# Reordering two stage boundaries in a fused adaLN + spectral mixer + MLP backward kernel

## The chip, the cores and the metric

The kernel runs on one core of one Trainium2 chip. The metric is device time in microseconds of one execution, the median of three runs. The engines are named as the profile names them: PE (matrix products), DVE (elementwise and reductions), ACT (activations and PSUM evacuation), POOL and SP (here mostly issuers of DMA). The program is written in Tile: instructions are traced in Python order, a planner puts them into one fixed order per engine from its own estimates, and every engine then runs its list in that order, waiting on semaphores. `issue_after(x)` forces instructions behind x in the list of their engine.

## The reference, cut to what matters

The forward pass is a conditioned block of two halves, and the kernel computes its output and the gradients of nine inputs. Sizes: 2048 tokens (S), 1024 channels (D), 3584 hidden (F), bf16.

```python
def _fwd_reference(A_x, A_w_r, A_w_i, B_x, B_w1, B_b1, B_w2, B_b2, c, w_mod):
    # A: rfft2 over (tokens, channels), times w_r + i w_i, irfft2
    # B: layernorm, gelu(y @ w1 + b1) @ w2 + b2
    ...
    mod = (_silu(c) @ w_mod).reshape(c.shape[0], 6, 1, -1)
    sa, ca, ga, sb, cb, gb = (mod[:, 0].copy(), ...)
    h = _layernorm(x, axis=-1) * (1 + ca) + sa
    x = x + ga * _A_ref(h, A_w_r, A_w_i)
    h = _layernorm(x, axis=-1) * (1 + cb) + sb
    x = x + gb * _B_ref(h, B_w1, B_b1, B_w2, B_b2)
    return x

def reference(..., grad_out):
    _out, _vjp = jax.vjp(_f, A_x, A_w_r, A_w_i, B_w1, B_b1, B_w2, B_b2, c, w_mod)
    return (_out, *_vjp(grad_out))
```

## The kernel before, in words

Tokens are worked on in four groups of 512, called frames or quarters here (b = 0 to 3), each held as four tiles of 128 tokens. All weights and the large intermediates pass through on-chip buffers that are named by a tag (`px0` to `px5`, `sma`, `smb`, `t0` to `t3`, `uv0` to `uv3`, `fr`, `ot`, `wt`, `ph`, `gm`, `sb`); a tag has one buffer, and a new tile of that tag waits until every reader of the old one is done. PSUM has the tags s and d (two banks each) and f (four banks).

The stages in order: modulation rows; the forward spectral mixer; the MLP, forward and its inner gradient; the backward of the second LayerNorms; the backward of the spectral mixer, with the weight gradients of w2 and w1 filled in as spare work for PE; the last sums.

The MLP works frame by frame. `z_block` (L795) forms the hidden pre-activations, applies gelu and its derivative, and stores two arrays to HBM: `d_hh` (hidden activations) and `d_gz` (gradient of the pre-activations). `bo_pass` (L836) multiplies by w2, in two column halves of seven steps each; a step is 16 matmuls and one w2 block of 512 KB, loaded into a ring of four buffers (`w2p`, L831). After the seventh step the four sums (`pbo`) are evacuated by ACT (L845), DVE forms the output and a product `go`, and PE sums it over tokens (`pa`, L855) into `gacc`. A plan written by hand sets PE's order here, and `ordered()` keeps it. The z blocks of a frame run among the steps of the frame before, so frame 3 has w2 steps alone. When frame 3 is done, `gacc` is reduced (`pq`, L903), stored as row 5 of the modulation gradient, and a ring of eight steps (`gmod_ring((5,))`, L958 and L960) turns it into one part of the gradient of w_mod.

The first boundary of this document, called seam 1, lies here. The next stage needs w1 transposed: seven tiles `w1T`, loaded by 28 transposing DMAs on SP (L973), each into the buffer of a spent w1 tile. Then, for every frame (L1002 to L1053 of the loop `for b in range(NB)`): load `n3u`, `n2u`, four tiles of grad_out (`go4`) and seven blocks of `gz` (L1013, a ring of eight buffers); the product `pg` = gz x w1T (L1020) in two column halves, evacuated by ACT into `gn3` (L1025, two buffers, so PE may be one frame ahead); then on DVE `ln_bwd` over `n3u` (L919 to L924), column sums of `gn3` and `pru` on PE (`sums3`), `ln_bwd` over `n2u`, adding `go4`, which gives g2. g2 is stored to `d_gx1` from POOL (L1046), multiplied by the ga row into `n3u`, folded over tokens and channels by eight half-width additions and subtractions into one quarter of `fbuf2`, and multiplied by `au` (a load of `d_A`) for another column sum, `sums3_ga` (L195).

The second boundary, seam 2, follows frame 3: four tiles `gB` = grad_out x gb row are loaded and multiplied (into `px2` to `px5`, the buffers of w1T tiles 0 to 3). Then `pieces()` hands out PE work: for each of 28 blocks of hidden units a transposing load of `d_hh` (L1139, two ahead) and two products gw2 (L1114) of 16 matmuls over all 16 token tiles, evacuated and stored as the gradient of w2; later the gradient of w1. `fill(n)` runs the next n of them: 16 of them stand before the spectral backward, whose first matmul is `pu` (L470) and needs all of `fbuf2`.

Of the kernel before, what the change touches and what calls it, by code (L numbers as in the profile page):

```python
# [14 lines left out]
ALU = mybir.AluOpType  # L15
# [20 lines left out]
def kernel(  # L36
# [69 lines left out]
    d_gx1 = dram.tile([S, D], BF16, name="d_gx1")  # L106
    d_ph = dram.tile([F, S], BF16, name="d_ph")
# [712 lines left out]
    w2n = [0]  # L820

    def bo_pass(b, h):
        cs_ = slice(h * KH, (h + 1) * KH)
        pbs = [(ps_f if b < NB - 1 or h == 0 else (ps_s, ps_d)[k % 2])("pbo") for k in range(4)]
        for i in range(4):
            with ordered():
                last_pe[0] = nc.tensor.matmul(pbs[i][:], lhsT=ones_bf[0:1, :], rhs=b2_row[0:1, cs_], start=True, stop=False)
        for g in range(7):
            wp = w2p[w2n[0] % 4]
            w2n[0] += 1  # L830
            nc.sync.dma_start(out=wp, in_=w2_v[:, g * 4:(g + 1) * 4, cs_])  # L831
            hh = hh_slots[(b * 7 + g) % 11]
            for i in range(4):
                for k in range(4):
                    with ordered():
                        last_pe[0] = nc.tensor.matmul(pbs[i][:], lhsT=hh[:, k, i * P:(i + 1) * P], rhs=wp[:, k, :],  # L836
                                                      start=False, stop=(g == 6 and k == 3))
# [12 lines left out]

        yield
        pa = (ps_d if b < NB - 1 else ps_f)("pa")
        for i in range(4):
            with ordered():
                last_pe[0] = nc.tensor.matmul(pa[32 * i:32 * (i + 1), :], lhsT=ones_bf[:, 0:32], rhs=go[:, i, :], start=True, stop=True)  # L855
# [42 lines left out]
    for late in bo_late:  # L898
        next(late, None)
    g5 = []  # L900
    for h in range(2):
        pq = (ps_s, ps_d)[h]("pq")
        nc.tensor.matmul(pq[0:1, :], lhsT=quad[:], rhs=gacc[:, h * KH:(h + 1) * KH], start=True, stop=True)  # L903
        g5.append(pq[0:1, :])
    store_gmod(g5, 5)

    gb1 = small.tile([P, NFC], FP32, tag="gb1", bufs=1)
    nc.vector.reduce_sum(out=gb1[:], in_=gb1_acc[:], axis=AX.X)
    gb1_bf = small.tile([P, NFC], BF16, tag="b1_bf", bufs=1)
    nc.vector.tensor_copy(out=gb1_bf[:], in_=gb1[:])  # L910
    fin = reg.tile([P, 2, P], BF16, name="fin", tag="gm")
    make_identity(nc, fin[:, 0, :])
    to_rows(fin[0:NFC, 1, :], gb1_bf[:], NFC, fin[:, 0, :])
    nc.sync.dma_start(out=out_5.rearrange("(f p) -> f p", p=P), in_=fin[0:NFC, 1, :])


    def ln_bwd(g_in, gsum, n_ap, rstd, out_ap, tmp):
        sc = small.tile([P, 4], FP32, tag="lbsc", bufs=4)
        nc.vector.tensor_tensor_reduce(out=tmp, in0=g_in, in1=n_ap, scale=1.0, scalar=0.0,  # L919
                                       op0=ALU.mult, op1=ALU.add, accum_out=sc[:, 1:2])  # L920
        nc.vector.tensor_scalar(out=sc[:, 2:3], in0=gsum, scalar1=rstd, scalar2=-1.0 / D, op0=ALU.mult, op1=ALU.mult)
        nc.vector.tensor_scalar(out=sc[:, 3:4], in0=sc[:, 1:2], scalar1=rstd, scalar2=-1.0 / D, op0=ALU.mult, op1=ALU.mult)
        nc.scalar.activation(out=tmp, in_=n_ap, func=ACT.Identity, scale=sc[:, 3:4], bias=sc[:, 2:3])
        nc.vector.scalar_tensor_tensor(out=out_ap, in0=g_in, scalar=rstd, in1=tmp, op0=ALU.mult, op1=ALU.add)  # L924
# [43 lines left out]
    w1Ts = []  # L968
    for g in range(7):
        wtile = reg.tile([P, 4, D], BF16, name=f"w1T_{g}", tag=W1T[g])  # L970
        for k in range(4):
            fc = g * 4 + k
            nc.sync.dma_start_transpose(out=wtile[:, k, :], in_=B_w1[:, fc * P:(fc + 1) * P])  # L973
        w1Ts.append(wtile)
    gzr = [reg.tile([P, 2, 4, BW], BF16, name=f"gzr{k}", tag=f"t{k}") for k in range(4)]
    gn3s = [reg.tile([P, 4, D], BF16, name="gn3a", tag="uv0"), reg.tile([P, 4, D], BF16, name="gn3b", tag="wt")]
    n3u = reg.tile([P, 4, D], BF16, name="n3u", tag="uv1")
    n2u = reg.tile([P, 4, D], BF16, name="n2u", tag="uv2")
    pru = reg.tile([P, 4, D], BF16, name="pru", tag="uv3")[:]
# [3 lines left out]
    gzn = 0  # L983
    gmw = reg.tile([P, 2, D], BF16, name="gmw", tag="ph")
    gmg = reg.tile([P, 2, D], BF16, name="gmg", tag="sb")
    early = gmod_ring((5,), [gmw[:, 0], gmw[:, 1], gmg[:, 0]], gmg[:, 1, :])
    next(early)
    au = reg.tile([P, 4, D], BF16, name="au", tag="px1")

    fold2_in = {}  # L990
# [9 lines left out]

    for b in range(NB):
        gn3 = gn3s[b % 2]  # L1002
        sums = small.tile([P, 2, 4], FP32, tag="sums")
        gzt = []
        nc.sync.dma_start(out=n3u[:], in_=chunk_rows(d_n3, b))
        nc.sync.dma_start(out=n2u[:], in_=chunk_rows(d_x1, b))
# [3 lines left out]
        for g in range(7):  # L1010
            sl = gzr[gzn % 8 // 2][:, gzn % 2]
            gzn += 1
            nc.sync.dma_start(out=sl, in_=d_gz_v[:, g * 4:(g + 1) * 4, b * BW:(b + 1) * BW])  # L1013
            gzt.append(sl)
        for h in range(2):
            pgs = [ps_f("pg") for _ in range(4)]
            for g in range(7):
                for i in range(4):
                    for k in range(4):
                        nc.tensor.matmul(pgs[i][:], lhsT=gzt[g][:, k, i * P:(i + 1) * P],  # L1020
                                         rhs=w1Ts[g][:, k, h * KH:(h + 1) * KH],
                                         start=(g == 0 and k == 0), stop=(g == 6 and k == 3))
            for i in range(4):
                with tc.high_priority():
                    nc.scalar.activation(out=gn3[:, i, h * KH:(h + 1) * KH], in_=pgs[i][:], func=ACT.Identity,  # L1025
                                         accum_out=sums[:, h, i:i + 1])
# [4 lines left out]
        next(early, None)  # L1031
# [12 lines left out]
        next(early, None)  # L1044
        tt(g2[:], g2[:], go4, ALU.add)
        nc.gpsimd.dma_start(out=chunk_rows(d_gx1, b), in_=g2[:])  # L1046
        nc.sync.dma_start(out=au[:], in_=chunk_rows(d_A, b))
        tt(n3u[:], g2[:], bcn(ga_row, 4), ALU.mult)
        fold_tok(n3u, ftmp)
        fold2_in[b] = fold_d(fbuf2[:, b], n3u[:], ftmp)  # L1050
        tt(au[:], g2[:], au[:], ALU.mult)
        if b < NB - 1:
            sums3_ga(b, au)  # L1053
            next(early, None)
# [3 lines left out]
    gBs = []  # L1058
    for b in range(NB):
        gb_t = reg.tile([P, 4, D], BF16, name=f"gB{b}", tag=PXT[2 + b])  # L1060
        gb_in = load_tok(gb_t, grad_out, b)
        with tc.high_priority():
# [15 lines left out]
    hh_o = [4, 5, 6, 7] * 2 + [0, 1] + [2, 0, 1] * 6  # L1078
# [32 lines left out]
    gwo = reg.tile([P, 2, D], BF16, name="gwo", tag="ph")  # L1111

    def gw2_mm(acc, fc, h, t):
        nc.tensor.matmul(acc[:], lhsT=hh_s[hh_o[fc]][:, t, :], rhs=gBs[t // 4][:, t % 4, h * KH:(h + 1) * KH],  # L1114
                         start=(t == 0), stop=(t == NT - 1))

    def gw2_out(acc, fc, h):
        with tc.high_priority():
            nc.any.tensor_copy(out=gwo[:, fc % 2, h * KH:(h + 1) * KH], in_=acc[:])  # L1119
        if h == 1:  # L1120
            nc.gpsimd.dma_start(out=out_6[fc * P:(fc + 1) * P, :], in_=gwo[:, fc % 2])

    w1g = {}
    hh_in = [None]
# [12 lines left out]
    def pieces():  # L1137
# [3 lines left out]
        hh_load(0)  # L1141
        yield
        hh_load(1)
        for fc in range(NFC):
            if fc + 2 < NFC:
                hh_load(fc + 2)
            for h in range(2 if fc < NFC - 2 else 0):
                acc = ps_f("gw2acc")
                for t in range(NT):
                    gw2_mm(acc, fc, h, t)  # L1150
                gw2_out(acc, fc, h)
# [38 lines left out]
    done = [0]  # L1190
# [6 lines left out]
    next(todo)  # L1197
    with tc.issue_after(gb_in.ins):
        fill(6)
# [81 lines left out]
```

## Time and profile before

| | us |
|---|---|
| median of 3 runs (1502.69 to 1513.5) | 1510.4 |
| the profiled execution | 1507.2 |
| its span in the trace | 1505.0 |
| PE busy | 1408.0 (94%) |
| DVE busy | 1068.8 (71%) |
| ACT busy | 721.4 (48%) |
| POOL busy | 371.6 (25%) |
| mean granted TensorE clock | 0.978 |
| last w2 step of the MLP begins | 768.0 |
| first `pg` matmul | 777.8 |
| last `pg` matmul ends, about | 988.9 |
| first `pu` matmul | 1062.6 |

The profile is one execution. It is read as a page of totals, and by queries of its trace: who waited for whom, the instructions in order of time, and the busy time of each engine in a stretch. An entry `x<-y` names what an instruction writes and reads; the bracket behind a timeline row is the idle time of the engine ahead of it and what ended that. Stretches with a clock under 1.00 are those in which PE had been idle.

### The profile page before, as it was taken

The page shows a single profiled execution, that of the slowest core. Times are in us where ns is not written, and L with a number is a line of the kernel's source. Part 1 is how long each engine was busy: PE and PEld are TensorE (multiplying, and loading weights), DVE is VectorE, ACT ScalarE, POOL GpSimd, SP SyncE. Part 2 cuts the span into 40 slices and gives each one's busy share as a digit, 9 for nine tenths or more (in the row PEclk, how much of TensorE's full clock was granted, in tenths as well). Part 3 has the DMA queues.
Part 4 walks back from the last instruction along what each step waited for, and adds up shares of the span by engine and source line. Part 5 has one row for each costly group of instructions (what it writes and reads, how often), then busy time and mean ns, then how long its engine had stood idle before and what let it go on. Part 6 is the DMA issues. An engine that isn't in the chain of part 4 may idle for free.

```text
span 1505.0 us, 18218 instructions
## 1 busy us (share of the span) xinstructions
PE 1408.0 (94%) x6703; PEld 655.0 (44%) x6835; DVE 1068.8 (71%) x1574; ACT 721.4 (48%) x960; POOL 371.6 (25%) x427
## 2 busy tenths in 40 slices
PE   5899989999999999999889999969999999899998
PEld 2434545444444444444334444424454444444443
DVE  5883777898799888877413877959067776997551
ACT  4765446757887755666111433313532344453211
POOL 5710631210112122212112001220124421222432
PEclk8999999999999999999999999989999999999999
DMA  9982664899687777899956246398379987675992
GB/s 336 265 223 67 156 212 137 264 245 338 225 252 230 233 243 231 247 279 262 344 195 221 76 180 224 107 214 211 98 188 241 248 221 222 175 198 149 275 294 92
DMA packets 358168, 324.27 MB, mean 215 GB/s; under 512 B 209191, under 2 KB 300861, under 8 KB 357824
## 3 DMA queue, kind: packets, MB, share of 16 engines
q1 hardware_dynamic: 324192, 207.71, 51.3%
q0 software_dynamic: 33888, 115.41, 22.5%
q8 instruction: 53, 0.87, 0.2%
q14 instruction: 35, 0.29, 0.1%
HBM read 164.15 MB, written 109.10 MB: 182 GB/s over the span
## 4 chain that ended last, share of the span: by engine, by line
PE 42%; DVE 19%; DMA 8%; issue 6%; ACT 5%; POOL 1%; SPq 0%; POOLq 0%; DVEq 0%; ACTq 0%
PE pbo L836 10%; PE pz L795 10%; PE gw2acc L1114 8%; PE gw1acc L1181 4%; PE pg L1020 4%; DVE ct L172 4%; DVE got L919 2%; PE pu L470 2%; PE pv L563 2%; ACT ct L460 1%; DVE gn3a L924 1%; DVE st L436 1%; DMA gB<-in_grad_out_dram 1%; DMA n3u<-d_n 1%; DMA w2sA<-in_B_w_dram 1%
## 5 line engine op out<-in xcount | busy, mean ns | idle before, releaser
L678 PE MATMUL pp<-gBoT,wt 128*128 128x512 bf16 x878 | 198.2, 383 | 4.9 <-DMA wt<-in_B_w_dram 2.0
L1020 PE MATMUL pg<-w1T,gzr 128*128 128x512 bf16 x876 | 195.2, 381 | 1.5 <-issue 0.7
L1181 PE MATMUL gw1acc<-gzh,n3n 128*128 128x512 bf16 x876 | 195.0, 381 | 1.1 <-issue 0.2
L678 PEld LDWEIGHTS <-wt 128*128 128x128 bf16 x896 | 88.0, 98 | 110.0 <-issue 6.1
L795 PEld LDWEIGHTS <-w 128*128 128x128 bf16 x896 | 87.5, 98 | 109.4 <-issue 6.0
L1020 PEld LDWEIGHTS <-gzr 128*128 128x128 bf16 x896 | 87.0, 98 | 108.5 <-issue 6.0
L1181 PEld LDWEIGHTS <-n3n 128*128 128x128 bf16 x896 | 87.6, 98 | 105.9 <-issue 2.4
L795 PE MATMUL pz<-n3Ta,w 128*128 128x512 bf16 x437 | 99.5, 383 | 2.9 <-ACT gt L798 2.1
L1114 PE MATMUL gw2acc<-gB,hhsA 128*128 128x512 bf16 x437 | 97.9, 379 | 1.0 <-DMA hhsA<-d_hh 0.4
L795 PE MATMUL pz<-n3Tb,w 128*128 128x512 bf16 x439 | 98.4, 379 | 0.5
L1119 ACT CAST gwo<-gw2acc 128x512 bf16<-128x512 f32 x54 | 30.5, 584 | 130.1 <-PE gw2acc L1114 84.1
L836 PEld LDWEIGHTS <-hhA 128*128 128x128 bf16 x608 | 58.9, 98 | 75.2 <-issue 5.1
L798 ACT ACTIVATE gt<-pz,b_col 128x512 bf16<-128x512 f32 x112 | 73.1, 683 | 35.6 <-PE pz L795 33.7
L1185 ACT CAST gwo<-gw1acc 128x512 bf16<-128x512 f32 x53 | 30.8, 582 | 115.1 <-PE gw1acc L1181 91.6
L804 ACT ACTIVATE gt<-gt 128x2048 bf16<-128x2048 bf16 x28 | 53.5, 1910 | 66.1 <-DVE gt L172 66.0
L172 DVE TENSOR_TENSOR gt<-gt,gt 128x2048 bf16<-128x2048 bf16 x56 | 68.5, 1223 | 21.6 <-ACT gt L806 20.9
L172 DVE TENSOR_TENSOR ct<-ct 128x2048 bf16<-128x2048 bf16 x64 | 75.9, 1221 | 10.3 <-ACT ct L631 9.0
L1114 PE MATMUL gw2acc<-gB,hht 128*128 128x512 bf16 x251 | 58.6, 393 | 14.4 <-DMA hht<-d_hh 10.3
L1114 PEld LDWEIGHTS <-hhsA 128*128 128x128 bf16 x448 | 43.6, 98 | 52.5 <-DMA hhsA<-d_hh 0.9
L800 ACT ACTIVATE gt<-gt 128x2048 bf16<-128x2048 bf16 x28 | 53.4, 1907 | 0.6
L806 ACT ACTIVATE gt<-gt 128x2048 bf16<-128x2048 bf16 x28 | 53.4, 1907 | 0.5
L1186 POOL DMA_DIRECT2D out_dram<-gwo x56 | 30.5, 546 | 84.5 <-ACT gwo L1185 74.3
(313 smaller groups left out, 2495.2 us busy)
## 6 DMA issues: line engine op xcount, KB each, us to landing
gzr<-d_gz SPq DMA_DIRECT2D x28, 512.0 KB, 6.4
wblk<-in_w_mod_dram SPq DMA_DIRECT2D x12, 1024.0 KB, 9.7
d_ph<-pho POOLq DMA_DIRECT2D x21, 512.0 KB, 5.6
out_dram<-otl POOLq DMA_DIRECT2D x40, 256.0 KB, 3.6
d_hh<-hhA POOLq DMA_DIRECT2D x19, 512.0 KB, 4.8
w2sD<-in_B_w_dram SPq DMA_DIRECT2D x14, 512.0 KB
hhC<-d_ph SPq DMA_DIRECT2D x14, 512.0 KB, 4.9
w2sA<-d_ph SPq DMA_DIRECT2D x14, 512.0 KB, 4.5
```

The costliest lines, as they stand in the source:

```text
L172: return nc.vector.tensor_tensor(out=out, in0=a, in1=b, op=op)
L678: last_pe[0] = nc.tensor.matmul(pp[:], lhsT=wt[:, fg % 2, cch, k * P:(k + 1) * P], rhs=gBoT[j][:, cch, :], start=(cch == 0), stop=(cch == ...
L795: last_pe[0] = nc.tensor.matmul(pz[:], lhsT=w1s[g][:, cch, k * P:(k + 1) * P], rhs=n3T[:, cch, :], start=(cch == 0), stop=(cch == NDC - 1))
L798: nc.scalar.activation(out=zb[:, k, :], in_=pz[:], func=ACT.Identity, bias=b1_col[:, fc:fc + 1], scale=1.0)
L800: nc.scalar.activation(out=av, in_=zb, func=ACT.Square)
L804: nc.scalar.activation(out=sg, in_=bv, func=ACT.Sigmoid, scale=2.0 * GK)
L806: nc.scalar.activation(out=bv, in_=bv, func=ACT.Sigmoid, scale=-2.0 * GK)
L836: last_pe[0] = nc.tensor.matmul(pbs[i][:], lhsT=hh[:, k, i * P:(i + 1) * P], rhs=wp[:, k, :], start=False, stop=(g == 6 and k == 3))
L1020: nc.tensor.matmul(pgs[i][:], lhsT=gzt[g][:, k, i * P:(i + 1) * P], rhs=w1Ts[g][:, k, h * KH:(h + 1) * KH], start=(g == 0 and k == 0), sto ...
L1114: nc.tensor.matmul(acc[:], lhsT=hh_s[hh_o[fc]][:, t, :], rhs=gBs[t // 4][:, t % 4, h * KH:(h + 1) * KH], start=(t == 0), stop=(t == NT - 1))
L1181: nc.tensor.matmul(acc[:], lhsT=n3ns[t // 4][:, t % 4, cch * P:(cch + 1) * P], rhs=gz2[t // 8][:, t % 8, :], start=(t == 0), stop=(t == NT ...
L1185: nc.any.tensor_copy(out=ob, in_=acc[:])
```

## The change

Four things are altered, all between the last MLP frame and the spectral backward.

Seam 1: the w2 loads of the last frame are issued three steps ahead; the transposes of w1T from number 8 on and the gz blocks of frame 0 are tied behind given w2 loads on SP; the `pg` product of frame 0 is written as two generators and its steps follow the last w2 step in PE's fixed order, the second column half in the s and d banks of PSUM, with the late `pa`, the `pq` reduction and the whole row-5 ring of the modulation gradient between them.

The frame loop: the ga product and the fold work in place in g2, not in `n3u`; the `au` column sum of a frame is issued on PE behind the next frame's `pg`; `gn3a` and `pru` exchange buffers (`uv3`, `uv0`).

gB: each frame multiplies its `go4` by the gb row once it is no longer needed. For frames 0 and 1 the product goes to a new HBM array `d_gB` and is loaded again at the end of frame 2, for frames 2 and 3 it goes straight into the tiles that the gw2 products read.

Seam 2: the first two transposed hh tiles are loaded into the quarter of `fbuf2` that the last frame will fill, and their four products run on PE directly behind the last `pg`.

```diff
+    d_gB = dram.tile([2 * BW, D], BF16, name="d_gB")
...
+    def w2_load(upto):
+        while len(w2_in) <= min(upto, NB * 14 - 1):
+            n = len(w2_in)
+            h, g = n // 7 % 2, n % 7
+            w2_in.append(nc.sync.dma_start(out=w2p[n % 4], in_=w2_v[:, g * 4:(g + 1) * 4, h * KH:(h + 1) * KH]))
...
-            wp = w2p[w2n[0] % 4]
-            w2n[0] += 1
-            nc.sync.dma_start(out=wp, in_=w2_v[:, g * 4:(g + 1) * 4, cs_])
+            n = (2 * b + h) * 7 + g
+            w2_load(n + 3 if b == NB - 1 else n)
+            wp = w2p[n % 4]
...
-        pa = (ps_d if b < NB - 1 else ps_f)("pa")
+        pa = (ps_f if (b, h) == (NB - 1, 0) else ps_d)("pa")
...
+    def behind_w2(k):
+        return tc.issue_after(w2_in[(NB - 1) * 14 + min(max(k, 0), 13)].ins)
+
+    for g in range(7):
+        wtile = reg.tile([P, 4, D], BF16, name=f"w1T_{g}", tag=W1T[g])
+        for k in range(4):
+            fc = g * 4 + k
+            with behind_w2(fc - 8) if fc >= 8 else ExitStack():
+                nc.sync.dma_start_transpose(out=wtile[:, k, :], in_=B_w1[:, fc * P:(fc + 1) * P])
+        w1Ts.append(wtile)
+        with behind_w2(11 + g):
+            load_gz(0, g)
...
+    pg0 = [pg_pass(0, 0, lambda k: ps_f, ordered), pg_pass(0, 1, lambda k: (ps_s, ps_d)[k // 2], ordered)]
+    for n, h in enumerate((0, 0, 0, 0, 1, 0, 1, 0, 1, 0, 1, 1, 1, 1)):
+        if n == 2:
+            for late in bo_late:
+                next(late, None)
+        if n == 4:
+            gmod5()
+        next(pg0[h])
...
+    hh_f = fbuf2[:, 3].rearrange("p (k a) (b f) -> p k (a b) f", k=2, f=P)
+    def hh_in_frame(fc):
+        hh_in[0] = nc.sync.dma_start_transpose(out=hh_f[:, fc], in_=d_hh[fc * P:(fc + 1) * P, :])
...
+        if b > 0:
             for g in range(7):
+                load_gz(b, g)
+            if b == 2:
+                hh_in_frame(0)
+                hh_in_frame(1)
+            for h in range(2):
+                for _ in pg_pass(b, h, lambda k: ps_f):
+                    pass
+            with tc.issue_after(last_pg[0].ins):
+                sums3_ga(b - 1, au)
+        gn3 = gn3_of(b)
+        if b == NB - 1:
+            gBs[3] = reg.tile([P, 4, D], BF16, name="gB3", tag="px5")
+            tt(gBs[3][:], go4, bcn(gb_row, 4), ALU.mult)
+            for fc in range(2):
+                for h in range(2):
+                    gw2_product(fc, h)
...
         nc.gpsimd.dma_start(out=chunk_rows(d_gx1, b), in_=g2[:])
+        if b < 2:
+            tt(go4, go4, bcn(gb_row, 4), ALU.mult)
+            nc.gpsimd.dma_start(out=chunk_rows(d_gB, b), in_=go4)
+        elif b == 2:
+            gBs[2] = reg.tile([P, 4, D], BF16, name="gB2", tag="px2")
+            tt(gBs[2][:], go4, bcn(gb_row, 4), ALU.mult)
+            for k in range(2):
+                gBs[k] = reg.tile([P, 4, D], BF16, name=f"gB{k}", tag=("px3", "px4")[k])
+                gb_in = nc.sync.dma_start(out=gBs[k][:], in_=chunk_rows(d_gB, k))
         nc.sync.dma_start(out=au[:], in_=chunk_rows(d_A, b))
-        tt(n3u[:], g2[:], bcn(ga_row, 4), ALU.mult)
-        fold_tok(n3u, ftmp)
-        fold2_in[b] = fold_d(fbuf2[:, b], n3u[:], ftmp)
         tt(au[:], g2[:], au[:], ALU.mult)
-        if b < NB - 1:
-            sums3_ga(b, au)
-            next(early, None)
+        tt(g2[:], g2[:], bcn(ga_row, 4), ALU.mult)
+        fold_tok(g2, ftmp)
+        fold2_in[b] = fold_d(fbuf2[:, b], g2[:], ftmp)
...
-    for b in range(NB):
-        gb_t = reg.tile([P, 4, D], BF16, name=f"gB{b}", tag=PXT[2 + b])
-        gb_in = load_tok(gb_t, grad_out, b)
-        with tc.high_priority():
-            with tc.issue_after(fold2_in[2].ins):
-                tt(gb_t[:], gb_t[:], bcn(gb_row, 4), ALU.mult)
-        gBs.append(gb_t)
...
-    hh_o = [4, 5, 6, 7] * 2 + [0, 1] + [2, 0, 1] * 6
+    hh_o = [None, None] + [4, 5, 6, 7, 4, 5] + [0, 1] + [2, 0, 1] * 6
...
-    next(todo)
     with tc.issue_after(gb_in.ins):
-        fill(6)
+        fill(2)
```

More of the change, by code (lines that the diff above doesn't have):

```diff
@@ L910 @@
[L910 to L924, printed above, removed]
+    w1Ts = []
@@ new lines, with gn3_of, load_gz @@
+    gzr = [reg.tile([P, 2, 4, BW], BF16, name=f"gzr{k}", tag=f"t{k}") for k in range(4)]
+    gzs, g_sums, gn3s = {}, {}, {}
+    def gn3_of(b):
+        if b % 2 not in gn3s:
+            gn3s[b % 2] = reg.tile([P, 4, D], BF16, name=f"gn3{'ab'[b % 2]}", tag=("uv3", "wt")[b % 2])
+        return gn3s[b % 2]
+    def load_gz(b, g):
+        n = b * 7 + g
+        gzs[b, g] = gzr[n % 8 // 2][:, n % 2]
+        nc.sync.dma_start(out=gzs[b, g], in_=d_gz_v[:, g * 4:(g + 1) * 4, b * BW:(b + 1) * BW])
@@ L966, in gmod_ring, with gmod5 @@
             yield
[L968 to L976, printed above, removed]
+    def gmod5():
+        g5 = []
+        for h in range(2):
+            pq = (ps_s, ps_d)[h]("pq")
+            with ordered():
+                last_pe[0] = nc.tensor.matmul(pq[0:1, :], lhsT=quad[:], rhs=gacc[:, h * KH:(h + 1) * KH], start=True, stop=True)
+            g5.append(pq[0:1, :])
+        store_gmod(g5, 5)
+        gmw = reg.tile([P, 2, D], BF16, name="gmw", tag="ph")
+        gmg = reg.tile([P, 2, D], BF16, name="gmg", tag="sb")
+        for _ in gmod_ring((5,), [gmw[:, 0], gmw[:, 1], gmg[:, 0]], gmg[:, 1, :]):
+            pass
```

130 lines of the change are left out of this document (68 added, 62 removed).

## The prediction

> **What bounds the kernel now.** I first cut the span into stages with the table of windows, since a whole-span share (PE busy 94%) says nothing about the two places that the change touches. Columns: stretch and its length, then busy time of PE, PEld, DVE, ACT and POOL, then granted TensorE clock, DMA share and GB/s.
>
> ```profile
> 713.70:767.00 53.30, 47.61 (x217) 20.50 (x221) 16.88 (x24) 6.92 (x8) 10.41 (x12) 1.00 1.00 325
> 767.00:801.00 34.00, 29.46 (x127) 12.06 (x128) 10.45 (x16) 6.56 (x8) 5.86 (x7) 0.95 0.42 141
> ...
> 878.20:932.20 54.00, 50.47 (x245) 22.49 (x249) 44.47 (x61) 19.39 (x28) 4.20 (x3) 1.00 0.46 165
> ...
> 988.90:1008.40 19.50, 5.43 (x13) 1.70 (x14) 6.85 (x5) 0.69 (x2) 3.52 (x1) 0.67 1.10 249
> ```
>
> The first two rows are seam 1 (last frame of the MLP, then the first `pg` product), the third is one of the frames between the seams, the last is seam 2, where PE works 5.4 of 19.5 us at clock 0.67. From 713.7 (first bias row of the last frame, L827) to 1062.6 (first `pu` of the spectral part, L470) PE is busy 315.0 of 348.9 us, so about 34 us can be won there and no more. Before 713.7 and after 1062.6 the instructions are the same in number and I leave both untouched.
>
> Second, PE's waits from 690 to 1070, the ones that matter (total, times, longest):
>
> ```profile
> PE gw2acc L1114 <- DMA hht<-d_hh: 10.3, 1, 10.3
> PE gw2acc L1114 <- DVE gB L172: 3.8, 2, 3.5
> PE acc3b L195 <- DVE au L172: 3.4, 3, 1.2
> PE pa L855 <- DVE otile L172: 2.6, 1, 2.6
> PE pbo L836 <- DMA w2sA<-in_B_w_dram: 2.5, 2, 1.8
> ```
>
> Seam 2 is a wait for loads (`hht`, `gB`), seam 1 a scatter of small ones. DVE too stands at seam 2: it multiplies one gB at 983.0 and waits 12.3 and 4.0 us for the loads of the others, so the last frame's LayerNorm backward, whose input left PE at 989.4, starts only at 1008.3.
>
> Third, DVE's and POOL's timeline at the end of one frame's backward, because the change rewrites just that:
>
> ```profile
> 858.87 2.29 DVE L172 TENSOR_TENSOR gn3a<-gn3a,got 128x4096 bf16<-128x4096 bf16 x1
> 861.20 2.29 DVE L172 TENSOR_TENSOR n3u<-gn3a,rows 128x4096 bf16<-128x4096 bf16 x1
> 863.41 2.29 DVE L172 TENSOR_TENSOR au<-gn3a,au 128x4096 bf16<-128x4096 bf16 x1
> ...
> 861.71 0.76 POOL L1046 DMA_DIRECT2D d_gx<-gn3a  x1 [44.26 <-issue]
> ...
> DMA to landing us min/median/max: 7.4/8.8/11.5
> ```
>
> The reader should see that g2 (`gn3a`) is ready at 861.16, its store to `d_gx1` leaves POOL at 861.71, and the last line (the four stores of L1046) says that it lands 7.4 to 11.5 us later; the one of 861.71 took 8.9. Today nobody waits for it, because the next line writes `n3u`.
>
> **Seam 1.** Today the last frame's 14 steps (16 matmuls, 3.456 us each by their starts) run from 716.98 to 771.65, then come the last evacuation, `pa` and `pq`, and `pg` of frame 0 ends at 828.4. Without stalls: 716.98 + 14 x 3.456 (48.4) + 2.3 for bias rows and `pa` = 767.7; with the last `pa` and `pq` placed between `pg` steps instead of ahead of them (0.9 and 1.5 with the evacuation of `pq`, which shares the s and d banks), 14 x 3.456 again gives 818.5. That is 9.9 us less. The 1.9 us wait for the evacuation at 713.7 is not touched.
>
> Whether the loads follow decides it. The 28 transposes of w1T are issued today from 622.9 to 718.1; the change ties number 8 and later behind the w2 loads of the last frame, so 17 fall after 713.7. In MiB from there until PE needs the last w1T tile: w2 5.5, gz 4, x1/grad_out/out halves 4.5, last stores of hh and gz 1.5, n3u and n2u 2: 17.5 MiB, at the 369 GB/s of 730 to 740 (no transpose there) 49.7 us. A transpose is bounded by its queue: 63.0 us of issue for 28 is 2.25 each; taking the plain bytes of 700 to 710 out of that slice (298 GB/s, 3.4 transposes) leaves 1.3. At 1.7: 28.9. With 5.4 to land, 84.0 us. PE reaches that tile after nine `pg` steps, 767.7 + 31.1 + 2.4 = 801.2, that is 87.5 after 713.7. So it just fits at 1.7, and at 2.25 PE would stall 5.9. I charge 2. A row of the modulation (`gmod5`, DVE steps 791.2 to 816.5 today, starting about as early after) ends where the backward of frame 0 now starts; that is in the same 2. The backward starts at T0 = 826.7 - 9.9 + 2 = 818.8.
>
> The Trainium skill (DMA: Bandwidth & Descriptors, Latency and other measured facts) gives a DMA transpose 261 GB/s. An estimate by that page: 256 KB in 1.0 us, 17 in 17, no charge and a forecast 2 us lower. The trace shows 256 KB per 2.25 us of queue, far slower, so the rows decide.
>
> **The frames between the seams.** Removed: PE's wait for `au` (1.1 to 1.2 each), since `sums3_ga` of the frame before goes behind the `pg` pass; and the wait for `n3u`, whose load can start after its first use (5.6 us twice on DVE, but PE had only finished at 879.1, so 1.6 each really). Added on DVE: the gB multiply, 2.2 (the four run at seam 2 today, so it is a move). Added as a wait: `g2 *= ga` in place may not overwrite g2 until the `d_gx1` store has read it. From 861.16 DVE has two operations to run (gB, `au`: until 865.6); the store lands at 870.6. Stall 5.0. With landing at 7.4 it is 3.5, at 11.5 it is 7.6; nothing (store read out early) is the lower bound. I take 5.0, the row of the same store in the same place. Queued behind the stalled multiply on DVE are the folds and the next frame's backward; PE waits for that at `sums3` a few us into the following pass. A DVE frame is 880.74 to 929.14 = 48.4 without the n3u wait, so 48.4 + 2.2 + 5.0 = 55.6, against 54.0 today: **these frames get 1.6 longer**, and DVE, not PE (50.7), sets them.
>
> **Seam 2.** gB of quarter 2 is multiplied from rows that are on chip, quarters 0 and 1 come back from `d_gB`, issued as soon as w1T tiles 1 and 2 are spent, some 15 us before the pass ends; a 1 MB load lands in 7.8 to 8.9 here. Quarter 3 needs go4, whose load waits for the quarter-2 multiply: 36.7 into frame 2's backward plus 8 to 10, then 2.2, against 55.6 for the frame. The hh tiles 0 and 1 lie in the frame buffer long before. So neither wait of seam 2 returns; if go4 takes the 17.4 us of today's gB load, 36.7 + 17.4 + 2.2 = 56.3 costs 0.7. Later hh loads sit behind gB on SP and have four products (13.8) of cover.
>
> The last backward starts at T3 = 818.8 + 3 x 55.6 = 985.6, plus 2.2 for gB of quarter 3, and runs 1008.3 to 1054.05 = 45.7 as today, plus its own store wait: 1040.36 + 7.4 = 1047.8 against 1042.3 when `au` is done, 5.5. Fold ends at 985.6 + 2.2 + 45.7 + 5.5 = 1039.0. PE: its pass ends 49.7 after T2 = 930.0, at 979.7; then 0.6, 16 products of 3.456 (as today between the seams' end and `pu`) and 1.0 of sums: 1036.6. DVE is later: `pu` starts at 1039.2.
>
> **Sum.** 1062.6 - 1039.2 = 23.4 us. The profiled execution took 1507.2 (span 1505.0), so 1483.8: 1484. The three runs shown have median 1510.4 and spread from 1502.7 to 1513.5; the profiled one is 3.2 below the median. About 1% is what this kernel's measurement can tell from nothing.
>
> **Rivals.**
> 1. *The store wait is not felt* (DMA reads g2 out sooner, or the queue is emptier now that go4 and `au` load at other times). For: 4 us slices around 866 show DMA share 1.06, so the 8.9 holds foreign traffic. Then PE sets frames at 50.7, T3 = 968.9 with T0 at 816.8, `pu` at 1026.4: 1471. Against: the gB store is added right there. 0.16.
> 2. *Half of the gain is given back*: transposes at 2.25 (3.9 more than charged), the store at 11.5 in all four frames (frame 58.2, last wait 9.6: T3 = 993.4, `pu` at 1051). The second alone gives 1496, both 1500. This is also where a gB of quarter 3 behind hh transposes ends. 0.22.
> 3. *Slower*: seam 1 becomes bound by the transposes. The stall is 49.7 + 17x + 5.4 - 87.5 = 17x - 32.4 for x us per transpose; it eats the gain from x = 3.4 and passes 1% slower at 4.3. For: the longest w1T issue is 4.95 and three hh transposes of twice the size took 20.43 (3.4 per 256 KB) beside other loads, and DMA share is already 1.0 or more here. At 4.95 the stall is 51.8 and the time 1534. Against: four beside two loads and a store took 9.27. 0.12.
> 4. *The change does not do what it says*: the planner leaves the products or loads of seam 2 late, and only seam 1 is won: DVE frames of 55.6 without the 17 us of seam 2 give some 1501; in rival 2's share of the chances.
>
> **How the numbers follow.** The forecast (1476 to 1493) has 0.50. Faster by over 1% (under 1492): the forecast nearly whole, rival 1, so 0.65; within 1%: 0.22; slower by over 1%: 0.13. The range runs from 1469, just below rival 1, to 1511, which covers rivals 2 and 4 and leaves most of 3 out.
>
> **What would show it.** Right: no `hht` or gB wait of PE over 2 us between the last `pg` and the first product; `pg` matmuls directly behind the last `pbo`; DVE waiting 3.5 to 7.6 for a `d_gx` DMA ahead of a `gn3` multiply in each frame; `pu` about 23 earlier. Wrong if PE waits for `w1T` or `gzr` at seam 1, if DVE frames stay below 52, or if the stretch after `pu` is no longer 442 us.

## The result, and the profile after

The changed kernel takes 1496.4 us (median; 1490.2 to 1499.5) against 1511.4 (1501.7 to 1513.6) for the kernel before on the same chip: a ratio of 0.991, 95% interval 0.989 to 0.994. It is faster by 0.9% where 1.8% was forecast. The profiled execution took 1498.7 with a span of 1496.9, against 1507.2 and 1505.0.

The first `pu` begins at 1054.1, 8.5 us earlier than before; the forecast had 1039.2, 23.4 earlier. From there to the end both kernels take the same, 442.8 and 442.4 us. So the missing 15 us lie between the last MLP frame and `pu`. The table of windows of the changed kernel (stretch and length, busy time of PE, PEld, DVE, ACT and POOL, granted clock, DMA share, GB/s) finds the place:

```profile
713.40:768.60 55.20, 53.02 (x237) 22.86 (x241) 16.94 (x23) 8.78 (x11) 10.27 (x12) 0.97 1.06 295
768.60:801.00 32.40, 32.24 (x146) 13.83 (x148) 5.72 (x6) 5.22 (x5) 3.96 (x4) 1.00 0.84 217
...
823.20:840.00 16.80, 0.23 (x3) 0.12 (x2) 11.26 (x26) 2.37 (x2) 2.69 (x5) 0.61 0.81 259
...
997.77:1054.11 56.34, 56.08 (x271) 25.32 (x273) 47.19 (x65) 17.66 (x25) 7.18 (x8) 1.00 0.64 170
```

Seam 1 (first two rows) is now full: PE works 53.0 of 55.2 and 32.2 of 32.4 us. So is the stretch from the first gw2 product to `pu` (last row), 56.1 of 56.3, where before PE worked 5.4 of 19.5 us at its start. The hole is new: from 823.2 to 840.0 PE does 0.23 us of work, at clock 0.61. PE's waits from 690 to 1070 (engine, tile and line, what it waited for; total, times, longest) name it:

```profile
PE acc3a L196 <- DVE gn3a L1033: 18.5, 2, 16.6
PE acc3a L196 <- DVE gn3b L1033: 2.6, 1, 2.6
PE pbo L834 <- ACT otile L852: 1.9, 1, 1.9
```

All waits of the kernel before are gone but the 1.9 us of `pbo`: no `hht`, no gB, no w2. In their place stands one wait of 16.6 us for DVE's backward of frame 0. The end of a frame's backward, on DVE's timeline, answers to the rows shown of before:

```profile
867.18 2.29 DVE L173 TENSOR_TENSOR gn3a<-gn3a,got 128x4096 bf16<-128x4096 bf16 x1
869.51 2.29 DVE L173 TENSOR_TENSOR got<-got,rows 128x4096 bf16<-128x4096 bf16 x1
871.72 2.28 DVE L173 TENSOR_TENSOR au<-gn3a,au 128x4096 bf16<-128x4096 bf16 x1
877.02 2.29 DVE L173 TENSOR_TENSOR gn3a<-gn3a,rows 128x4096 bf16<-128x4096 bf16 x1 [3.02 <-DMA d_gx<-gn3a]
...
888.88 1.22 DVE L1028 CUSTOM_DVE_ANT_0 got<-gn3b,n3u 128x1024 bf16<-128x1024 bf16 x1
```

The reader should see the gB multiply (`got<-got`), the `au` multiply, and then the in-place multiply, which waits 3.02 us for the store to `d_gx`. After the fold the next frame starts at once at 888.88: the wait for `n3u` of 5.6 us that stood there is gone.

Why the backward of frame 0 starts late is seen on two timelines. First DVE, around the ring of modulation row 5:

```profile
784.87 0.68 DVE L178 CAST row<-pq 1x512 bf16<-1x512 f32 x1 [0.18 <-PE pq L999]
813.27 1.23 DVE L984 CUSTOM_DVE_ANT_0 gmw<-gmw,gmg 128x1024 bf16<-128x1024 bf16 x1 [27.72 <-DMA gmg<-d_gmod]
...
834.15 1.22 DVE L1028 CUSTOM_DVE_ANT_0 got<-gn3a,n3u 128x1024 bf16<-128x1024 bf16 x1
```

The row is ready at 785.55. The ring that uses it starts at 813.27, after 27.7 us of idle time, takes 20.9 us (25.3 in the kernel before), and ends only when the backward of frame 0 (`got<-gn3a`) can begin, at 834.15. DVE runs its list in order and the ring is ahead of the backward, whose own input had left PE at 819.4. Second SP, which stores the row and loads it back to all partitions:

```profile
781.89 0.45 SPq L1084 DMA_DIRECT2D n3u<-d_n  x1
782.44 0.76 SPq L1086 DMA_DIRECT2D n2u<-d_x  x1
796.50 0.37 SPq L128 DMA_DIRECT2D got<-in_grad_out_dram  x1
796.92 3.27 SPq L1048 DMA_TRANSPOSE fbuf<-d_hh  x1
800.28 0.53 SPq L1135 DMA_DIRECT2D au<-d_A  x1
800.87 0.35 SPq L179 DMA_DIRECT2D d_gmod<-row  x1
...
801.76 7.33 SPq L1048 DMA_TRANSPOSE fbuf<-d_hh  x1
809.19 0.53 SPq L976 DMA_DIRECT2D gmg<-d_gmod  x1
```

The row's store stands at 800.87, behind the load of `got`. That load waited 13.1 us, by the profile for the scattered stores of `otile`, whose buffer (tag `ot`) `got` takes over. Behind it come a transposing load of hh (3.27 us of issue), `au`, and only then the store of 2 KB; then a second hh transpose holds the queue for 7.33 us before the row can be loaded back at 809.19. In the kernel before, SP issued the same store and load ahead of `got`:

```profile
782.86 0.31 SPq L178 DMA_DIRECT2D d_gmod<-row  x1
787.91 0.35 SPq L950 DMA_DIRECT2D gmg<-d_gmod  x1
794.88 0.38 SPq L127 DMA_DIRECT2D got<-in_grad_out_dram  x1
```

The change wrote the row reduction between the `pg` steps, and in SP's order its DMAs came out behind the first loads of the next stage.

### The profile page after: what moved, and what is told of

It reads as the page before. It is cut to its first block, busy times and chain, and to the rows that moved or that the text cites. A ratio compares the mean times of both kernels' runs of the same rounds, so it can differ in the third digit from the quotient of the medians.

```text
span 1496.9 us, 18191 instructions
## 1 busy us (share of the span) xinstructions
PE 1407.9 (94%) x6703; PEld 655.5 (44%) x6835; DVE 1069.7 (71%) x1574; ACT 721.7 (48%) x960; POOL 359.1 (24%) x421
## 5 line engine op out<-in xcount | busy, mean ns | idle before, releaser
L940 PE MATMUL pg<-w1T,gzr 128*128 128x512 bf16 x876 | 199.1, 386 | 1.3 <-issue 0.4
L173 DVE TENSOR_TENSOR gt<-gt,gt 128x2048 bf16<-128x2048 bf16 x56 | 68.5, 1223 | 21.6 <-ACT gt L807 20.9
L1065 PE MATMUL gw2acc<-gB,otl 128*128 128x512 bf16 x187 | 44.0, 390 | 3.5 <-DMA otl<-d_hh 2.0
```

What stands on the lines that cost most here:

```text
L173: return nc.vector.tensor_tensor(out=out, in0=a, in1=b, op=op)
L940: last_pg[0] = nc.tensor.matmul(pgs[i][:], lhsT=gzs[b, g][:, k, i * P:(i + 1) * P], rhs=w1Ts[g][:, k, h * KH:(h + 1) * KH], start=(g == 0 ...
L1065: nc.tensor.matmul(acc[:], lhsT=hh_of(fc)[:, t, :], rhs=gBs[t // 4][:, t % 4, h * KH:(h + 1) * KH], start=(t == 0), stop=(t == NT - 1))
```

## The experiments

Four numbers carry all runs. T0 is the start of the backward of frame 0 on DVE; it is given from the end of the last w2 step, which itself varies by a few microseconds from run to run. Each row is the profiled execution of the kernel, with the median of its runs in the first column.

| kernel | median | ring starts | last w2 step to T0 | T0 to `pu` | `pu` to end |
|---|---|---|---|---|---|
| before | 1511.4 | 791.2 | 55.1 | 235.9 | 442.4 |
| changed | 1496.4 | 813.3 | 65.4 | 220.0 | 442.8 |
| e1, row ahead of got and hh | 1493.0 | 797.5 | 57.7 | 219.8 | 444.1 |
| e2, row ahead of hh alone | 1498.3 | 810.3 | 62.0 | 219.6 | 443.7 |
| e4, without the ring | 1488.5 | none | 48.9 | 220.2 | 449.0 |
| e11, SP cleared for the row | 1486.6 | 794.7 | 52.4 | 219.0 | 443.7 |
| e8, all but seam 1 | 1500.1 | 794.8 | 56.4 | 221.8 | 447.0 |
| e9, seam 1 alone | 1510.2 | 807.0 | 60.5 | 234.0 | 449.3 |
| e7, fold not in place | 1515.4 | 812.0 | 64.5 | 234.7 | 442.9 |
| e5, fold without the store wait | 1494.2 | 815.5 | 64.7 | 213.8 | 443.8 |
| e12, gB of quarter 3 loaded | 1501.3 | 815.2 | 65.6 | 220.3 | 446.1 |
| e10, e11 and e5 together | 1483.2 | 793.3 | 52.7 | 214.2 | 447.1 |

The kernel before, beside e1, e2, e4 and e8, took 1510.7; beside e5, e9, e10 and e11 1510.0; beside e7 and e12 1508.6.

### Is it the row? The ring left out, and the row's DMAs moved forward

**e4** leaves the ring out: the reductions, scalings and w_mod loads of row 5 are replaced by zeros, so one row of the gradient of w_mod and its part of the gradient of c are not computed. It bounds what the row can cost.

```diff
-        for _ in gmod_ring((5,), [gmw[:, 0], gmw[:, 1], gmg[:, 0]], gmg[:, 1, :]):
-            pass
+        nc.vector.memset(gu[:, 5, :], 0.0)
+        nc.vector.memset(gmg[:, 1, :], 0.0)
+        ...
```

> The changed kernel without the work of the row-5 ring: its eight reductions, eight scalings and eight loads of w_mod are left out (that part of the gradients of w_mod and c is then not computed, zeros are stored). This bounds what the ring can cost. Theory A: frame 0's backward starts when PE delivers, at 817 to 819, and the time is the first experiment's within 3 us (some 1481). Theory B: also fast, so this one and the first one differ by 10 us or more. Theory C: pu within 4 us of 1054.

DVE's waits from 780 to 825 in this kernel show what sets T0 when there is no ring:

```profile
DVE got L1030 <- ACT gn3a L948: 32.1, 1, 32.1
```

It waits for the evacuation of `pg`, that is for PE. T0 is 48.9 us behind the last w2 step, 16.5 less than with the ring. That is the whole shortfall of 15 us. The time is 1488.5 us (ratio 0.984, interval 0.982 to 0.986), 8 below the changed kernel, where some 1481 were expected. In the profiled execution `pu` starts 13.6 us earlier, but the stretch behind it, which the edit doesn't touch, is 6 us longer.

**e1** ties the load of `got` and the two hh transposes behind the row's load on SP; **e2** ties the hh transposes alone (the last two lines of the diff).

```diff
+            row_in[r] = nc.sync.dma_start(out=gr, in_=d_gmod[r * D:(r + 1) * D].partition_broadcast(P))
...
+        with tc.issue_after(row_in[5].ins) if b == 0 else ExitStack():
+            load_tok(go4, grad_out, b)
...
+                with tc.issue_after(row_in[5].ins):
+                    hh_in_frame(0)
+                    hh_in_frame(1)
```

> The changed kernel, with two things tied on SP behind the load of the row-5 gradient (gmg <- d_gmod): the grad_out load of frame 0 and the two hh transposes into the frame buffer. Theory A (order on SP): in the changed kernel the row was ready on DVE at 785.6, but its store stood on SP behind the grad_out load (let go at 796.5) and a transpose of 3.3 us, and the load back behind a second transpose of 7.3 us; so the row-5 ring began on DVE at 813.3 instead of some 794, and the backward of frame 0, behind it on DVE, at 834.2 instead of 818. With the order mended the ring begins at 793 to 797, takes 21 us as before, frame 0's backward starts at 816 to 819, and with the 220 us from there to the first pu matmul of the changed kernel that one starts at 1036 to 1039: 15 to 18 us faster than the changed kernel, some 1481. Theory B (traffic): the row is late because the DMA engines are full of transposes and gz blocks; then the order hardly matters, the ring begins at 806 or later, and the gain over the changed kernel is under 5 us. Theory C (PE sets the frames and the late backward is absorbed): DVE starts earlier, but pu stays within 4 us of 1054.

> As the first, but only the two hh transposes are tied behind the row-5 load; the grad_out load of frame 0 keeps its place. Theory A: the store of the row still waits until 796.5 + 1, the load back is issued some 5 us later and lands at about 806, frame 0's backward starts at about 827: 7 us faster than the changed kernel, about half of the first experiment's gain. Theory B: as the first, under 5. Theory C: nothing.

e2 missed: counted from the last w2 step, the ring starts 5.3 us earlier and T0 comes 3.4 us earlier, where 7 were expected; its time, 1498.3 us (ratio 0.992, interval 0.990 to 0.994), is that of the changed kernel. The two transposes are not the main part of the delay. e1 comes close to where the ring was expected to start (797.5, against 793 to 797) but wins only half of T0: 57.7 us behind the last w2 step, 1493.0 us (ratio 0.989, interval 0.987 to 0.991), where some 1481 were expected. SP's timeline of e1 shows a part of the rest:

```profile
781.05 0.41 SPq L1086 DMA_DIRECT2D n3u<-d_n  x1
781.56 1.29 SPq L1088 DMA_DIRECT2D n2u<-d_x  x1
783.94 0.37 SPq L1139 DMA_DIRECT2D au<-d_A  x1
784.65 0.25 SPq L179 DMA_DIRECT2D d_gmod<-row  x1
...
793.45 0.34 SPq L978 DMA_DIRECT2D gmg<-d_gmod  x1
```

The row now leaves at 784.65, but the load that needs it is issued only at 793.45, 8.8 us later, with three loads of 1 MB (`n3u`, `n2u`, `au`) issued just ahead of the store. DVE also waited 11.3 us in the middle of the ring, for the second set of w_mod columns. Their load stands on SP behind `got` and the hh transposes, and the expectation of e11 blames these. But by SP's waits the load is released by the store of the first set from the same buffer (`gmw`), and in e11, where neither stands ahead of it, DVE still waits 9.7 us.

**e11** clears SP for the row: `n2u` of frame 0 behind the row's load (`gr_in`), and `got`, `au` and the hh transposes behind the last w_mod load of the ring (`row_in`).

```diff
+        with tc.issue_after(hh_in[0].ins) if b == NB - 1 else tc.issue_after(gr_in[5].ins) if b == 0 else ExitStack():
             nc.sync.dma_start(out=n2u[:], in_=chunk_rows(d_x1, b))
...
+        with tc.issue_after(row_in[5].ins) if b == 0 else ExitStack():
+            load_tok(go4, grad_out, b)
...
+                with tc.issue_after(row_in[5].ins):
+                    hh_in_frame(0)
+                    hh_in_frame(1)
...
+        with tc.issue_after(row_in[5].ins) if b == 0 else ExitStack():
+            nc.sync.dma_start(out=au[:], in_=chunk_rows(d_A, b))
```

> The changed kernel with SP's list cleared for the row-5 ring: n2u of frame 0 behind the load of the row, and au and grad_out of frame 0 and the two hh transposes behind the last load of the ring. In the first experiment the row still took 8.8 us to land behind 3 MB of n2u, n3u and au, and the second set of the ring waited 11.3 us behind grad_out and the hh transposes. Theory A (order and what stands ahead of the row in the queue): ring begins at 791 to 794, ends at 812 to 816, frame 0's backward starts when PE delivers, at 817 to 820, pu 220 later, at 1037 to 1040, some 1482. Theory B (the engines are busy with gz and w1T in any order): no better than the first experiment, start at 825, some 1491.

```profile
785.50 0.25 SPq L179 DMA_DIRECT2D d_gmod<-row  x1
789.77 0.35 SPq L978 DMA_DIRECT2D gmg<-d_gmod  x1
790.21 0.38 SPq L1088 DMA_DIRECT2D n2u<-d_x  x1
...
815.93 0.42 SPq L128 DMA_DIRECT2D got<-in_grad_out_dram  x1
```

These rows of SP in e11 show the store at 785.50 and the load at 789.77, 4.3 us apart, with `got` late at 815.93, where nobody misses it. T0 is 52.4 us behind the last w2 step, 13.0 less than in the changed kernel and 3.5 more than without the ring (e4). PE's wait of 16.6 us has shrunk to 3.6, and `pu` starts at 1040.1, against 1039.2 in the forecast. The time is 1486.6 us (ratio 0.985, interval 0.981 to 0.989). Nothing but the order of a few DMAs on SP was changed, no work was taken away. So by the medians the order of SP cost the changed kernel some 10 us, and with the order mended the forecast's sum is met.

### What each part is worth

**e9** makes the seam 1 change alone (with the row between the `pg` steps), frames and seam 2 as before; **e8** undoes seam 1 and keeps frames and seam 2.

```diff
 e8
-            w2_load(n + 3 if b == NB - 1 else n)
+            w2_load(n)
...
-    pg0 = [pg_pass(0, 0, lambda k: ps_f, ordered), pg_pass(0, 1, lambda k: (ps_s, ps_d)[k // 2], ordered)]
...
+    gmod5()
 e9
-            for fc in range(2):
-                for h in range(2):
-                    gw2_product(fc, h)
...
+        tt(n3u[:], g2[:], bcn(ga_row, 4), ALU.mult)
+        fold_tok(n3u, ftmp)
+        fold2_in[b] = fold_d(fbuf2[:, b], n3u[:], ftmp)
...
+        gb_in = load_tok(gb_t, grad_out, b)
```

> Seam 1 as in the changed kernel with the row-5 ring there; frame loop, fold into n3u, gB loads at the end and hh loads as in the kernel before (only gn3a and pru keep the exchanged buffers). Theory A (the late start of frame 0's backward decides): DVE starts it at 832 to 836, the rest runs as before but 6 to 9 us later, pu at 1068 to 1072: 5 to 9 us SLOWER than the kernel before although PE ends the first pg pass 9 us earlier. Rival (what PE wins at seam 1 is won for the kernel): 8 to 10 us faster than before.

> The frame loop and seam 2 as in the changed kernel, seam 1 undone: transposes and gz blocks of frame 0 without ties, w2 loads one step ahead, pg of frame 0 behind the last pa, the row-5 ring stepped in the frame loop. Theory A: frame 0's backward starts as in the kernel before, at 825 to 829, 6 to 9 us earlier than in the changed kernel though PE delivers 10 us later, and pu 220 us after it, at 1045 to 1049: 5 to 9 us FASTER than the whole change, some 1491. Theory C (PE sets the pace): 10 us slower than the whole change, some 1508.

e9 takes 1510.2 us, ratio 1.001 (0.999 to 1.003): neither the loss nor the gain that was expected. In its trace the two cancel: DVE waits 22.5 us for the row, less than the 27.7 of the changed kernel and as long as in e2 (22.4), where no hh transposes stand between either, and T0 comes 5.4 us later behind the last w2 step than before, which uses up what PE won ahead of it. Its waits show seam 2 untouched (DVE's from 780 to 1070, then PE's from 700 to 1110):

```profile
DVE gmw L984 <- DMA gmg<-d_gmod: 22.5, 1, 22.5
DVE got L1028 <- DMA n3u<-d_n: 11.3, 2, 5.9
```

```profile
PE gw2acc L1065 <- DVE gB L173: 9.4, 3, 6.5
...
PE gw2acc L1065 <- DMA hht<-d_hh: 1.6, 1, 1.6
```

e8 takes 1500.1 us (ratio 0.991, interval 0.987 to 0.994). T0 is at 830.1, a little behind what was expected, since its w2 steps wait 4.8 us in all for their loads; T0 to `pu` is 221.8. So nearly the whole measured gain is there without seam 1. What seam 1 as built adds, 1500.1 to 1496.4, is less than these runs can tell from nothing (e8's lie between 1490.6 and 1500.9). With SP's order mended (e11) `pu` comes 11.9 us ahead of e8's, and the medians are 1486.6 and 1500.1.

**e7** undoes the fold in place alone: the ga product goes to `n3u` again.

```diff
-        tt(g2[:], g2[:], bcn(ga_row, 4), ALU.mult)
-        fold_tok(g2, ftmp)
-        fold2_in[b] = fold_d(fbuf2[:, b], g2[:], ftmp)
+        tt(n3u[:], g2[:], bcn(ga_row, 4), ALU.mult)
+        fold_tok(n3u, ftmp)
+        fold2_in[b] = fold_d(fbuf2[:, b], n3u[:], ftmp)
```

> The fold in place undone, all else as changed: g2 times ga goes to n3u again, so no multiply waits for the d_gx1 store, and the load of n3u for the next frame has to wait for the folds again. Theory (in place trades one wait for the other): the four store waits of the changed kernel, 3.02 + 2.78 + 1.99 + 7.10 = 14.9 us on VectorE, go, and the wait for n3u of 5.6 us that the kernel before shows comes back ahead of frames 1, 2 and 3, 16.8 us. From the first backward to the first pu 220.0 - 14.9 + 16.8 = 221.9 us, no wait for d_gx, and a time within 3 us of the changed kernel's 1496.4. Rival (in place is a loss): n3u's load finds less traffic than before, waits under 2 us, the stretch takes 206 to 211 us and the time is 1483 to 1488. Other rival (in place is where the gain is): the stretch takes over 228 us and the time is over 1504.

This was the largest surprise: 1515.4 us (ratio 1.007, interval 1.004 to 1.009), slower than the kernel before and, by the medians, 19 above the changed one. The third of the theories held. DVE's waits from 885 to 1020:

```profile
DVE got L1028 <- DMA n3u<-d_n: 20.5, 3, 7.5
DVE gB L173 <- DMA got<-in_grad_out_dram,xu: 5.0, 1, 5.0
```

The loads on SP and the start of the next backward on DVE, in e7 and then in the kernel before:

```profile
881.03 0.37 SPq L128 DMA_DIRECT2D got<-in_grad_out_dram  x1
...
883.09 0.37 SPq L1084 DMA_DIRECT2D n3u<-d_n  x1
...
893.02 1.23 DVE L1028 CUSTOM_DVE_ANT_0 got<-gn3b,n3u 128x1024 bf16<-128x1024 bf16 x1 [7.51 <-DMA n3u<-d_n]
```

```profile
872.78 0.37 SPq L1005 DMA_DIRECT2D n3u<-d_n  x1
...
880.74 1.23 DVE L919 CUSTOM_DVE_ANT_0 got<-gn3b,n3u 128x1024 bf16<-128x1024 bf16 x1 [5.59 <-DMA n3u<-d_n]
```

The load of `n3u` is issued when the fold has read it for the last time, at the same place within the fold in both kernels. But the next backward starts 9.9 us after this in e7 and 8.0 in the kernel before, so DVE waits 7.5 us instead of 5.6. In e7 the load of `got` goes out 2.1 us ahead of that of `n3u`, in the kernel before 11.6 us; that this is the reason was not tested. The wait stands ahead of all three later frames, also ahead of the last one (5.9), where in the kernel before the wait of seam 2 covered it. And `got` comes 5.0 us late for the last gB. The last backward so starts 15.1 us later than in the changed kernel. Then PE waits 5.8 us for DVE's product `pru` in the last sums and has 35.2 us of products behind them, so `pu` starts only 6.9 us after the fold has ended. T0 to `pu` is 234.7 us, as long as before the change: **without the fold in place, nothing is left of what the frames and seam 2 gained.**

**e5** keeps `n3u` free but takes the store wait away: the ga product goes to the scratch tile and g2 serves as scratch, so g2 is overwritten one operation later (in the last frame `n3u` is the scratch).

```diff
+        ft2 = g2[:] if b < NB - 1 else n3u[:]
+        tt(ftmp, g2[:], bcn(ga_row, 4), ALU.mult)
+        fold_tok(ftmp, ft2)
+        fold2_in[b] = fold_d(fbuf2[:, b], ftmp, ft2)
```

> The changed kernel, but the ga product is written into the scratch tile of the fold and g2 serves as the fold's scratch (in frame 3 n3u does): the same instructions, the first that overwrites g2 comes one operation (2.2 us) later, in frame 3 never. DVE's waits for the d_gx1 store of the changed kernel (3.0, 2.8, 2.0 and 7.1 us, sum 14.9) should fall to 0.8, 0.6, 0 and 0. Theory A (DVE's chain from frame 0's backward to the end of the last fold sets pu): frame 0's backward still starts at about 834; the chain shrinks from 220 by 13.5 to 206.5, until PE's own list takes over (three passes of 50.7, 16 products and sums behind the late start, pu at about 1045). So 8 to 10 us faster than the changed kernel, some 1489. If the waits were covered by PE anyway: within 2 us of the changed kernel.

```profile
875.96 2.28 DVE L173 TENSOR_TENSOR pru<-gn3a,rows 128x4096 bf16<-128x4096 bf16 x1
878.66 2.36 DVE L173 TENSOR_TENSOR gn3a<-pru 128x2048 bf16<-128x2048 bf16 x2 [0.42 <-DMA d_gx<-gn3a]
...
888.35 1.23 DVE L1028 CUSTOM_DVE_ANT_0 got<-gn3b,n3u 128x1024 bf16<-128x1024 bf16 x1
```

These rows of DVE in e5 show the product at 875.96 without a wait, and 0.42 us left at the next operation. T0 to `pu` falls by 6.2 us to 213.8, though of the store waits of 14.9 us only 1.1 are left. The 7.1 of the last frame bring nothing, because there PE's own chain ends as late: in the changed kernel PE runs from 997.77 to `pu` without a gap while DVE's fold ends at 1054.07. In e5 the fold ends at 1041.9 and `pu` starts at 1049.7. The time is 1494.2 us (ratio 0.990, interval 0.986 to 0.994), 2 below the changed kernel, where 8 to 10 were expected.

**e12** loads the grad_out rows of quarter 3 a second time instead of using those on chip.

```diff
-            tt(gBs[3][:], go4, bcn(gb_row, 4), ALU.mult)
+            load_tok(gBs[3], grad_out, b)
+            tt(gBs[3][:], gBs[3][:], bcn(gb_row, 4), ALU.mult)
```

> Quarter 3 of gB from a load of its own into its own buffer instead of from the grad_out rows that are on chip; the buffer comes free with the last use of its w1T tile, at the end of the last pg pass. Theory (keeping rows on chip is what clears seam 2): the load starts at the end of the pass, lands 8 to 11 us later, VectorE multiplies it in order ahead of the last backward, so the last backward starts 8 to 10 us later (1000.2 to about 1009 in the profiled execution), TensorE waits for gB in the first product, and the time is 8 to 10 us above the changed kernel: 1504 to 1507. Rival (the load is hidden by the first product and by TensorE's other products): TensorE waits under 3 us, the first pu starts within 3 us of the changed kernel's, and the time is within 3 us of 1496.4.

The load on SP, then the multiply on DVE and the start of the last backward:

```profile
989.31 0.37 SPq L128 DMA_DIRECT2D gB<-in_grad_out_dram  x1
```

```profile
999.17 2.29 DVE L173 TENSOR_TENSOR gB<-gB,rows 128x4096 bf16<-128x4096 bf16 x1 [2.73 <-DMA gB<-in_grad_out_dram,xu]
...
1003.65 1.22 DVE L1028 CUSTOM_DVE_ANT_0 got<-gn3b,n3u 128x1024 bf16<-128x1024 bf16 x1
```

The buffer came free with a w1T tile that the pass was done with, so the load went out at 989.31, ten microseconds ahead of the end of the pass at 999.57, and the multiply waited 2.7 us for it, where it waits 1.7 for `got` in the changed kernel. PE has no gB wait at all. T0 to `pu` is 220.3: the rival held in the trace, and this part of the change is worth no more than 0.3 us there. The time, 1501.3 us (1497.9 to 1505.9; ratio 0.995, interval 0.992 to 0.997), is 5 above the changed kernel, where the rival had it within 3; in the profiled execution that difference lies in stretches that the edit doesn't touch (T0 comes 2.7 us later, `pu` to the end takes 446.1), and the intervals overlap.

**e10** is e11 and e5 together.

> Both: SP's list cleared for the ring and the fold's buffers swapped. Theory A: start at 817 to 820, DVE's chain 206.5 (pu at 1025), PE's list from 819.3: three passes of 50.7, then 0.6, 55.3 and 1.0: 1028. So PE sets it, pu at 1027 to 1031, some 1473 to 1476, faster than before by over 2%.

1483.2 us (1479.0 to 1483.6; ratio 0.982, interval 0.978 to 0.986): the fastest here, below both kernels. `pu` starts at 1034.4, 5.8 ahead of e11, but the stretch behind it took 447.1, 3.4 longer than in e11, and the expected 1473 to 1476 was missed. What the stretch ahead of `pu` still holds is nearly all PE's own work, as the windows show:

```profile
820.00:978.00 158.00, 151.98 (x722) 66.93 (x735) 140.91 (x188) 58.06 (x83) 15.01 (x14) 0.98 0.67 199
978.00:1034.40 56.40, 56.14 (x272) 25.37 (x274) 46.75 (x64) 17.87 (x25) 12.58 (x13) 1.00 0.71 198
```

PE is busy 152.0 of 158.0 us from T0 to the products and 56.1 of 56.4 behind them.

## Why the prediction was right or wrong

**The failed step** is the last term of seam 1: "A row of the modulation (`gmod5`, ...) ends where the backward of frame 0 now starts; that is in the same 2." Without that charge T0 was 816.8; it came at 834.15, so the term of 2 us measured 17.4. Within it the w1T transposes, for which the 2 was really meant, cost nothing. The row's DVE steps were moved with their durations, 25.3 us, and their start was taken to be "about as early after". The steps took less, 20.9 us, but they started at 813.3 instead of 791.2: what stood ahead of the row's two DMAs on SP was not asked. Counted from the last w2 step, 13.0 us of the delay go with SP's order alone (e11), and 3.5 more with the ring itself (e4). The before trace showed the danger: `got` waiting on SP until 794.88 with the row's store 12 us ahead of it. With T0 at 834.15 in the forecast's own sum, `pu` comes at 834.15 + 220.4 = 1054.5; it came at 1054.1. That this is so close is in part luck, as two errors behind T0 cancel (below).

**Right, seam 1 on PE.** The last w2 step was to end at 767.7 and `pg` of frame 0 at 818.5; they ended at 768.8 and 819.4. PE waits for no w1T, gz or w2. The third rival, bound by transposes, is dead: the 28 issues have a median of 1.63 us, the 1.7 that was taken. By an estimate from the figure of the Trainium skill (DMA: Bandwidth & Descriptors, Latency and other measured facts: 261 GB/s with a non-contiguous middle dimension, 1.0 us for 256 KB) no charge was due, and none came, though the issues measured here are longer than that.

**Right in sum, by errors that cancel: the frames.** Three DVE frames were to take 55.6 each and the gB multiply of quarter 3 another 2.2, 169.0 in all; they took 54.7, 54.2 and 57.1, 166.1, and the third of them already holds that multiply and its wait of 1.7. The store waits in them were 3.0, 2.8 and 2.0 and not 5.0, below the bound of 3.5, because the store landed 7.0, 6.8 and 5.9 us after its issue. The last backward with its fold was to take 51.2 and took 53.8; its store wait was 7.1 and not 5.5. So 2.9 us too many stand against 2.6 too few. DVE was to end 2.4 us after PE; the two came out level, at 1054.07 and 1054.11. The first rival, no store wait, is out as built; e5, which takes nearly all of these waits away, shows what it would be worth, 6 us and not 13, since the last wait lies beside PE's chain.

**Right in size, but for a wrong reason, the fold in place.** The text weighed it as 1.6 us lost per frame. e7 shows it as the part that the rest stands on: in the new order a fold through `n3u` makes frames of 59.2 and 58.2 and a T0 to `pu` of 234.7. The comparison was made with the old frame's 54.0, not with the old fold inside the new frame.

**Right, seam 2.** No `hht` or gB wait came back, and PE goes from the last `pg` into the products. e12 shows that keeping quarter 3 on chip is not what achieves this; the step "the buffer in time" held even for a load.

**The second rival** named the time, 1496 to 1500, but not the cause, so its hit is luck: neither were the transposes at 2.25, nor the store at 11.5. The fourth is out, since the order came out as written for seam 2. The test that `pu` to the end stays 442 held for the changed kernel (442.8).

## What to carry to other kernels

When a step is moved, follow its smallest DMAs through the queue of the engine that issues them: an instruction in that list that waits for a buffer holds all behind it. Here a 2 KB store stood behind a load that waited 13.1 us, and that order cost some 10 us by the medians. Judge an edit inside the new order, not against the old one: the fold in place looked like a small loss by the old frame, and in the new one the stretch from T0 to `pu` is 14.7 us longer without it. A load put into a buffer that comes free during a product may be as good as keeping the data.

## What the runs showed of the hardware

A row of 1024 values stored to HBM and loaded back by the same queue took, from the issue of the store to the issue of the load that waits for it, 3.6 us in e10, 4.3 in e11 and 5.1 in the kernel before, but 5.5 in e9 and 6.3 in e2, behind the loads of `got` and `au`, and 8.8 in e1 with three loads of 1 MB issued just ahead. A transposing load of 512 KB of hh held SP for 3.3 us in one case (changed kernel) and 10.6 in another (e11, beside the loads of `got` and `au`). The stretch from `pu` to the end, with the same work in all, took 442.4 to 449.3 us from kernel to kernel; the long ones show a little more PE work time and mostly longer waits for `ct`. In the traces of the four longest (e4, e8, e9, e10) the granted clock is at half for 17.9 to 21.7 us of this stretch, in the others for 8.4 to 15.8. Which comes first was not settled. Differences of 5 us between these kernels must therefore be read from the stretches and not from the totals.
